# A new emission order for a fused attention and Fourier-filter kernel: same operations, other order, other PSUM banks, other clamp pairs

## The chip, the cores and the metric

One core of one Trainium2 chip runs the whole program. The metric is the device time of one execution in microseconds (us); the median of several runs is compared. The profile is one execution taken by the hardware profiler. Its engines are PE (TensorE matmul; PEld its weight loads), DVE (VectorE), ACT (ScalarE), POOL (GpSimd) and SP (SyncE, which here only issues transfers).

## The reference

One batch of 2048 tokens, 448 features, bf16. Two branches of the same input are mixed by a gate for each token.

```python
x = A_x                                                   # [1, 2048, 448]
g = sigmoid((x * gate_w).sum(-1, keepdims=True))
q, k, v = split(x @ wqkv)                                 # 16 heads of 28
a = (softmax(q @ k.T * 28**-0.5) @ v) @ wo                # full attention
X = rfft2(x.astype(f32), axes=(-2, -1)) * (w_r + 1j * w_i)
b = irfft2(X, s=(2048, 448)).astype(bf16)
return g * a + (1 - g) * b
```

## The kernel before, in words

**Attention.** Four heads make a group `g`, 512 queries a block `c`; the 16 pairs (g, c) are worked off in a fixed sequence `n` = 0 to 15. For a pair, 16 key tiles `kt` of 128 keys are scored: a score matmul is [32 rows] x [128 keys x 512 queries], on one of four row tiles of TensorE (one for each head `s`), into one PSUM bank. A unit is one (n, kt, s).

There are two ways from a score to a probability. Most key tiles ("a" tiles) take ACT: one `ACTIVATE` of line 1111 takes the exponential of two units at once (128x1024) into a slot pair of `ring`. I call one such pair a step; there are 374, numbered 0 to 373, all two units wide. The last 3 to 5 key tiles of a pair ("d" tiles) take DVE and POOL: score matmuls named `dunit`, then a clamp on DVE (line 1061, `dp1`) that writes bf16 bits as integers into `pd`, then three `int64_add` on POOL (line 1075, `dexp`) that make three phase-shifted copies. A clamp takes one unit, or a pair of units in neighbouring banks; `PARTS` lists the ways in which the four units of a d tile can be split, and one byte of the table picks one for each of the 69 d tiles.

A `pv` operation is four matmuls on the four column tiles of TensorE (values x probabilities), added up in one PSUM bank `pvb`. When a pair (g, c) is done, `normalise` copies the bank out (line 1241), and a chain of small transfers and a reciprocal brings the row sums back for the last multiplication (line 1253): transfer 0 (`rs`), reciprocal, transfer 1 (`rsc`), four broadcasts 2 to 5 (`Rb`). For n = 15 that is done on TensorE instead.

**The rest**, fed in between: transposes of x (`x_block`), projections (`proj_group`; the squared norms go to `nrow` and by a small transfer into a row of `k` or `q`; in each of them a matmul `:4` makes the norms), values (`v_block`), their weights (`w_block`), and the Fourier branch: `fwd`, `fwd2`, sixteen `mid` (each loads seven pieces, `CS` and six of `Wg`), sixteen `inv` (each loads `V`). Then sixteen output tiles: `out_tile` 0 to 11 and `last_tile` 12 to 15, each eight column-tile operations (four of the Fourier branch, four of the attention), an eviction, and a store. `out_tile` t writes one of two buffers `fin`, so its eviction waits until the store of tile t-2 has landed.

Seven PSUM banks (`ps`) are handed out one by one to scores, clamps and the rest; the eighth is `pvb`.

**What sets the order.** `Sched.run` emits the operations in the order of a table. The engines work in program order, so the table fixes the order on each engine's queue (PE, DVE, ACT, POOL, and SP's transfer queue); waits between engines follow from the data. `TABLE` holds four compressed strings: `codes` (the operations' numbers in order of emission), `banks` (the PSUM bank for each item), `widths` (units in a step) and `parts` (the split of each d tile). `Kernel.passed` tells the framework which of the earlier `dexp` instructions a new clamp or `dexp` need not depend on ("product done": the `pv` that read it has passed).

Some names of the diff and of the text: `S` a score, `D` a dunit, `P` a pv operation, `O` an output-tile operation, `i` one of `inv`, `J` a projection. "Row work" is S and D (row tiles), "column work" is P, J, `fwd`, `mid`, O (column tiles), "full" are `v_block`, `inv` and transposes (the array as one tile).

Of the kernel before, what the change touches and what calls it, by code (L numbers as in the profile page):

```python
# [21 lines left out]
S, D, H, DH, F = 2048, 448, 16, 28, 225  # L22
# [16 lines left out]
    "eNoN14MCIDoSRNEkHXNs27Zt27Zt27Zt27Zt2zbe7P5E1bkKtUQaGdQUORQFRUXRUHQUA8VEsVBsFAchFBfFQ/FRApQQJUKJURKUFGGUDKVDyVF2"  # L39
    "lAJZlBLlQAR1RRJ5JBCg9CgVYigrSo0iIY6qozQoA0qLqqEaqArKgjKhnKgyiohyocwoG6qFMqLiqASKjEqimig3Ko0CioDKoLooD8qL8qECKD8q"  # L40
    "gsqiUqg8KogKocKoKNqEyqHNqAIqhlqhtmgL2opWonZoG9qOVqHVqBLagdagiWgtqogmocloHVqPpqCpaAPaif5jf9lv9ottRBTVQfVQQ9QbNUI9"
    "0TTUEXVC7VEz1AI1QVVRG9Qc/WH/2HQ0A81Es9BsNAfNRfPQfLQALUSL0GK0BC1FsXBsHAcvQ3FxPBwfJ8AJ8S4UEUfCkXEUHBVHw9FxDLwcJcIx"
    "8QqEOeK70R60F+1D+9EBRDnwp+gZeo5eoJfoFXqN3iDOBX+LCGdc8oNIc8UdtzzwCPwQuoPuonvoPnqAHqJH6DEy3POIPDFOgpPiZPgJeofeow/o"
    "I0qOP6HPqLarjQ6jSDwyj8qj8al4Gp6OZ+CYPAafiaPw6LyBPoKOomPoOPqC6uo4PDaPxU+guDwF/opS4ng8Pk/IE/E6OgFPzFPhU+g0OoPOonPo"
    "PLqALqJL6DK6gq6ia+g6uoFuom8oNW6MTqLW6Ba6jZLwpLwULo3L4BQ8OU/NU/GyOBlPydPgtDgd/o5+oJ/oF0qPf6MMuBwuj5vqhjoRJIa0PB2v"
    "pyvgNDwmZOAZeXRIzzPxxroijgFZeGbeXCeAyJCdZ+NZeQ4eCxJCR9wJ5+I5eVTojLvgKBANuuK8PA9PArl5Pp4ZZ8FZcTacHefAOXEunJ8X4PEg"
    "KVTC9VF8+Iv+oIy4D8qEu6G4EAeSQXJIAbEhN86D8+J8OD8ugAviQvg/9A8V4oU5whgTDJjigrwIL8qL8eI8PTDMscASK6yxwRY7XBgXwUVxBvA4"
    "4Ai4BC/Ju+MeuDQvw8vznrgXLsXL8nK8Iq/EW+u2ugTujUvi4rgYrsKr8pa6Mm6vq+CquBquwCvzarwGr85TQ21ek7fSzXRaqMWb6EY6DVTH6aAe"
    "r8tTQjaowzvoBjwHNOTtdAtdnzfi2SEVZIEmvDEfiUfhnJAVauBmvDnPBaPxGJwbmvI2uiVvxVvw1rwm7qjH4va8LW/DO/D6uh3vyGvhOrgurofr"
    "48yQFzqgfNALZYKM0Bn1QHmgC+qkB+rCUAg68068AS4CfXRvXQK68a68lquNO+suvDsfrofqHrwnLwd9dWUoCVWgD+/Nh+lBeoDuxfvy8lAV+vMy"  # L50
    "0I/31wP5IF4A8sMAPkIP1kP4UN5Fl4WC0Bq3wSP4cD6YD+MjeSloi9vhhjCKj+ZjeHEoDRWgPR6nG8EQPUrXh3F8LK8Bdd0EPpHXc/VdA1cJuqMG"
    "UBPG80l8Cp/MZ/GZvKFr5Bq7hrir7qZ76Gi+p+6ue+mxehqfzifoqXwGn80b4ca4KW6GW7vmeA6fyxtDG9cEWuCRuiIUhfm8BSzg8/gU3U8v5ot4"
    "NRitx+upeppuiRfyJbwDbgmtcHVYxpfyutAGVvCVvJ1r7ybpDq6jm6g1LOf1oC2s4+v5ar6GT9ar+Fq+gReDMbo21IHmUAuaQjPo5Dq7Pni6boIb"
    "oBm6rYvqB+MheCgehofjLq6J28g38c28qWvmmrtluh1s5Vv4Ar1Ud4UdfDtfqVfrbbyFa+m6Q3to5XrALr6br9HdoCfs5Hv4Pr6X7+etYJFerA/w"
    "g/wQbw393Qbd1XWGI/wwH+C6OQNdYKHu4Xq6Xu44P8YHwlG+RC/XJ3l/OMV7uxP8NF+hz/IzvBseBH3xWt3HDYC+rh/u587zC3yQG+xW6SFuqDvH"
    "L/NL/CK/yq/xK/w6H+PGunFuvNuuF+JFeDFegoe54W6Em+AmuknuJr/BB8NS3Ac6QS/oABv1Jn2b3+EjYQTs0lv0Zn2L3+X3+H0+BEbBHXwX38P3"
    "8QP8kD/iT/kT/hA/wo/xE/wUP8PP8Qv8Er/Cr/ED/pg/4yvwSrwKr8Zr8Fq8Dq/HG/BGvAlvxlvwVrwNb8fP+QveF17ycXimtjACO3iDZ+EdeDye"
    "gF/zV3winoT7wWQ80o1y7/hbPgne8Pd8r96mx8JH/oHv0Ov0ZJgCX/g0+Mw/8a98HEyH5bgjDIXesFOv18NgOHzj3/lomAFTYQzMhN36F//Jt+p9"
    "eo+egifCeJgDE+AH/83/8b/8D18MszES8+G//4/Nfj0HL4AlcEJf0QuBCBCn9Dl9Us8FJrg4qxc4KhbBGpBCCSG0WOgWucXuop4Ha2EFWGHEDX1Z"
    "n9FeBLEdnIgglriVsNQtc9PcdDfDzXSbIaKIJHbAbX1aRxFRxTqILKKJKH4Axr4/nqUj+9l6jp6rB+LubgGejwfhufiAnqfn4b9utFsKy2EWzIZl"  # L60
# [64 lines left out]
    "w33y7uZf/hf7bvjyhBu8Ts6vfm85QIy/yMohVurrn72vq8u7v1dD/uk4+uRxIJ9chFrL5Xf6RQGPIbgOoXupUuXjTCymQQNFr2kowqRmG0XzoPHS"  # L125
    "i6JBSQbcGfFk5AzRG6MnJOUndz09Msq5d8QGMkUpGDANHy/OD6bzDdc=",
# [1419 lines left out]
```

## Time and profile before

| | |
|---|---|
| median of 3 runs | 380.56 us (380.28 to 380.94) |
| the profiled execution | 380.92 us, span 379.0 us |
| first ACT step starts, last one ends | 12.67 us, 365.58 us |
| ACT line 1111 | 374 instructions, busy 345.6 us, idle before them 7.3 us |
| PE busy | 367.8 us (97%) |
| DVE busy | 336.6 us (89%) |
| POOL busy | 234.9 us (62%) |
| granted clock | 0.999 |

How to read it: a step of ACT lasts 1.02 us or more in the records, but the next one begins before it ends, so the pace is read from starts, not from durations. The same holds for PE: the ends of matmuls are modelled, and the distance of starts tells what an operation costs. The span lies 1.9 us below the profiled execution's own time, and that execution lies 0.36 us above the median.

### The profile page before, as it was taken

Reading aid. Unit: us, or ns where it says so; the run is one execution under the profiler, and the core shown is the slowest. Engines: PE = TensorE matmul, PEld = TensorE weight load, DVE = VectorE, ACT = ScalarE, POOL = GpSimd, SP = SyncE. Lnnn points to the kernel's source line nnn. Section 1 sums busy time; section 2 is a strip of 40 time slices with the busy share of each in tenths; the row PEclk is TensorE's granted clock in tenths of the full one; section 3 lists DMA queues with packets and bytes.
Section 4 is the critical chain, followed back from the end, with each engine's and each line's share of the span. In section 5 each row is a group of like instructions: output and inputs, shape, how many; then the busy total and the mean of one; then the engine's idle time right before and its main releaser. Section 6 shows DMA issues by size and latency. Waiting matters only on the chain.

```text
span 379.0 us, 12133 instructions
## 1 busy us (share of the span) xinstructions
PE 367.8 (97%) x5093; PEld 144.0 (38%) x5093; DVE 336.6 (89%) x649; ACT 350.6 (92%) x389; POOL 234.9 (62%) x264
## 2 busy tenths in 40 slices
PE   8999999999999999999999999999999989999995
PEld 5644233343333332334334434233333333433563
DVE  1769889999999999999999999999999989996644
ACT  2799999999999999999989999999999999999741
POOL 4707295747878876483463556877877759654610
PEclk9999999999999999999999999999999999999999
DMA  6601001001201122113211212212313222222122
GB/s 145 171 3 45 3 5 47 21 6 39 60 15 31 47 57 52 51 38 99 68 38 39 70 36 73 59 39 64 80 41 80 66 48 80 70 67 72 48 78 88
DMA packets 31154, 21.20 MB, mean 56 GB/s; under 512 B 16260, under 2 KB 29052, under 8 KB 31100
## 3 DMA queue, kind: packets, MB, share of 16 engines
q1 hardware_dynamic: 29708, 19.96, 20.0%
q8 instruction: 40, 0.66, 0.7%
q10 hardware_dynamic: 1392, 0.46, 0.5%
q14 instruction: 14, 0.11, 0.1%
HBM read 14.51 MB, written 1.96 MB: 43 GB/s over the span
## 4 chain that ended last, share of the span: by engine, by line
PE 49%; ACT 41%; DVE 5%; SPq 1%; issue 1%; DMA 1%; POOL 0%; DVEq 0%; POOLq 0%
ACT ring L1111 41%; PE ps L500 32%; PE pvb L500 16%; DVE pd L1061 3%; SPq L475 1%; PE ps L503 1%; DMA out_dram<-wpk 1%; DVE X L1373 0%; DVE pvs L1241 0%; DVE t L1437 0%; DMA Wg<-in_B_w_r_dram 0%; ACT V L1321 0%; DVE wpq L1299 0%; DVE wpk L1299 0%; DVE Ab L1390 0%
## 5 line engine op out<-in xcount | busy, mean ns | idle before, releaser
L1111 ACT ACTIVATE ring<-ps 128x1024 bf16<-128x1024 f32 x374 | 345.6, 1135 | 7.3 <-PE ps L500 7.1
L1075 POOL INT64_ADD pd<-pd x207 | 213.0, 1044 | 107.2 <-DVE pd L1061 32.3
L1061 DVE TENSOR_SCALAR pd<-ps 128x512 uint16<-128x512 f32 x260 | 177.2, 715 | 6.1 <-PE ps L500 3.8
L500 PE MATMUL ps<-q,k 32*128 32x512 bf16 x1024 | 143.7, 382 | 4.3 <-ACT ring L1111 1.5
L500 PE MATMUL pvb<-pd,vd 128*32 128x512 bf16 x1104 | 94.8, 384 | 0.0
L500 PEld LDWEIGHTS <-k 32*128 32x128 bf16 x1024 | 40.9, 91 | 118.1 <-issue 113.2
L500 PE MATMUL pvb<-ring,vw 128*32 128x512 bf16 x748 | 68.8, 384 | 0.4 <-DVE pvs L1241 0.4
L500 PEld LDWEIGHTS <-vd 128*32 128x32 bf16 x1104 | 24.3, 95 | 33.1 <-issue 27.8
L500 PEld LDWEIGHTS <-vw 128*32 128x32 bf16 x748 | 17.5, 94 | 25.3 <-issue 22.4
L500 PEld LDWEIGHTS <-xT 128*128 128x128 bf16 (+5 forms) x512 | 19.4, 97 | 10.8 <-issue 9.9
L1437 DVE TENSOR_TENSOR t<-ps,Wg 128x450 bf16<-128x450 f32 x32 | 19.0, 619 | 1.5 <-PE pvb L500 1.0
L500 PE MATMUL ps<-xT,wpq 128*32 128x512 bf16 (+3 forms) x248 | 19.4, 382 | 0.3 <-DVE wpq L590 0.3
L500 PE MATMUL ps<-xT,wpk 128*32 128x512 bf16 (+3 forms) x244 | 18.4, 383 | 0.0
L1373 DVE TENSOR_TENSOR X<-ps,oc 128x226 bf16<-128x226 f32 (+1 forms) x32 | 12.2, 385 | 0.6
L500 PE MATMUL ps<-wvr,xT 128*128 128x112 bf16 (+1 forms) x192 | 12.7, 213 | 0.0
L500 PEld LDWEIGHTS <-CS 128*32 128x32 bf16 x384 | 8.8, 95 | 9.5 <-issue 5.2
L804 DVE TENSOR_SCALAR q<-ps 128x512 bf16<-128x512 f32 x15 | 10.3, 684 | 2.3 <-PE ps L500 2.3
L500 PE MATMUL ps<-wpk,q 128*32 128x448 bf16 x128 | 11.7, 362 | 0.0
L500 PE MATMUL ps<-wpq,q 128*32 128x448 bf16 x128 | 11.5, 362 | 0.0
L500 PE MATMUL ps<-Bd,xT 128*32 128x226 bf16 (+2 forms) x256 | 11.1, 263 | 0.3 <-ACT ring L1111 0.3
L1494 DVE TENSOR_TENSOR X<-ps,ogb 113x512 bf16<-113x512 f32 x16 | 10.3, 674 | 1.2 <-PE ps L500 1.2
L804 DVE TENSOR_SCALAR k<-ps 128x512 bf16<-128x512 f32 x15 | 10.3, 684 | 0.9 <-PE ps L500 0.8
(99 smaller groups left out, 270.5 us busy)
## 6 DMA issues: line engine op xcount, KB each, us to landing
Rb<-rsc SPq DMA_DIRECT2D x60, 64.0 KB
CS<-cCS SPq DMA_DIRECT2D x16, 192.0 KB
V<-xtok SPq DMA_DIRECT2D x16, 113.0 KB
Wg<-in_B_w_i_dram SPq DMA_DIRECT2D x64, 28.1 KB
xtok<-Ab SPq DMA_DIRECT2D x16, 112.5 KB
xtok<-in_A_x_dram SPq DMA_DIRECT2D x3, 448.0 KB
Wg<-in_B_w_r_dram SPq DMA_DIRECT2D x32, 28.1 KB
out_dram<-wpq SPq DMA_DIRECT2D x6, 112.0 KB
```

The costliest lines, as they stand in the source:

```text
L475: self.pin(e.dma_start(out=out() if callable(out) else out, in_=in_() if callable(in_) else in_))
L500: self.pin(self.nc.tensor.matmul(out, lhsT=lhsT, rhs=rhs, start=start, stop=stop, **kw))
L503: self.pin(self.nc.tensor.transpose(out=out, in_=in_, identity=self.c("ident")[0:n, 0:n]))
L804: self.pin(nc.vector.tensor_scalar(out=dst, in0=self.bgi(it), scalar1=SQ, scalar2=None, op0=ALU.mult))
L1061: self.pin(nc.vector.tensor_scalar(out=free_dims(ys[:], [[512 * e, w], [1, 512]], 512 * part[0]).bitcast(U16), in0=self.ps[:, bs[0]:bs[0] ...
L1075: self.pin(nc.gpsimd.int64_add(out=fl(pds), in0=fl(ys), in1=PHASE[f] * 0x0001000100010001))
L1111: self.pin(nc.scalar.activation(out=self.ring[:, u0:u0 + len(st), :], in_=self.ps[:, bs[0]:bs[0] + len(st), :], func=ACT.Exp, scale=LN2 / ...
L1373: self.pin(nc.vector.tensor_tensor(out=free_dims(self.X1[:, t, :], [[F, 2], [-1 if dif else 1, n]], (F - 1) * dif), in0=free_dims(self.bgi ...
L1437: self.pin(nc.vector.tensor_tensor(out=out[:], in0=self.bgi(it)[:, 0:F2].rearrange("p (a f) -> p a f", a=2), in1=free_dims(Wg[:], [[F, 2], ...
L1494: self.pin(nc.vector.tensor_tensor(out=free_dims(self.zt[0:FN], [[128, 4], [1, 128]], 512 * t), in0=self.bgi(it)[0:FN, :].rearrange("p (a ...
```

## The change

The source is the same but for the table and one condition in `passed`:

```diff
 TABLE = (
-    "eNoN14MCIDoSRNEkHXNs27Zt27Zt27Zt27Zt2zbe7P5E1bkKtUQaGdQUORQFRUXRUHQUA8VEsVBsFAchFBfFQ/FRApQQJUKJURKUFGGUDKVDyVF2"
...
+    "eNoN14MCIDoSAMFkYq9t27Zt27Zt27Zt27Zt28bbu6+oboVaIo0MaoocioKiomgoOoqBYqJYKDaKgxCKi+Kh+CgBSogSocQoCUqKMEqG0qHkKDtK"
...
     "eNpjYhoF9AcAJW4C7Q==",
-    "eNpjYGBgYGRgYWDgBBF4AAsnUAkEcHBycrKBGBABFhYACYkAYw==",
+    "eNoti0EOACAMwrpkc/L/DytTAqEHgIQJwShlfz0I6k7a2FtoSU25fI08EEkArQ==",
 )
@@ passed
-                                       keep=[p for p in self.copies if self.taken.get(p.name, o.at) >= o.at])
+                                       keep=[p for p in self.copies
+                                             if p is self.before.get(ins.engine) or self.taken.get(p.name, o.at) >= o.at])
```

Decompressed and read against the list of operations, the tables say this. `widths` is the same string: 374 steps of two units, so ACT's work is the same. `parts` differ: 54 d tiles of 69 were clamped unit by unit before, 41 are after; 260 clamps (244 of one unit, 16 of two) become 245 (214 and 31). All other operations are the same set, 3997 before and 3982 after. The first 69 PE operations and the first 12 transfers of SP are the same. ACT's order differs only in where seven small instructions stand (the weights' exponentials). On PE 2026 of 2377 operations stand at another place, by 3 places in the median and 90 at most; on SP 283 of 316.

Runs of row work on PE (stretches of S and D with nothing else between) are 328 before and 322 after. By stretches of steps, counted in the emission order from the last score of one step to the last score of another:

| steps | row runs before / after | column operations | full operations |
|---|---|---|---|
| 0 to 8 | 5 / 6 | 13 / 11 | 48 / 55 |
| 8 to 64 | 49 / 51 | 113 / 114 | 60 / 56 |
| 64 to 152 | 83 / 80 | 199 / 202 | 69 / 69 |
| 152 to 193 | 34 / 37 | 101 / 97 | 36 / 36 |
| 193 to 208 | 11 / 12 | 43 / 46 | 27 / 20 |
| 208 to 312 | 95 / 92 | 202 / 202 | 73 / 80 |
| 312 to 320 | 8 / 7 | 18 / 17 | 0 / 0 |
| 320 to 360 | 37 / 36 | 85 / 84 | 48 / 48 |
| 360 to 373 | 7 / 6 | 68 / 63 | 12 / 12 |

PE near the last steps, before (the number after S is the step):

```
i(4) P O4(0-7) i(8) S363 S364 P O3(0-7) P P P S365 S366 D D O6(0-7) P S367 D D P P O5(0-6) S368 S369
O8(0-5) P O5(7) O8(6-7) O10(0-2) P S370 S371 O7(0-3) O10(3) O7(4) O10(4) P O7(5) P O10(5-7) S372 S373 ...
```

and after:

```
i(12) P P O4(0-5) S363 S364 O4(6-7) P P O3(0-7) S365 S366 D D P P O6(0-7) P S367 S368 D D P O5(0-3) P O5(4-7) P S369 S370 S371
P O10(0-2) P P O10(3-5) O7(0-7) O10(6) S372 S373 ...
```

Behind step 373 PE has 18 `out_tile` operations and 7 pv operations left before, 25 and 6 after; the `last_tile`, `inv` and `normalise` operations there are the same.

SP's queue after its twelfth transfer, before: `wk` part 2, `wq` part 2, `A`, `wk` part 1, the norm row of k block 1, k block 2, k block 3, ... After: one `Wg` piece and the `CS` of `mid` 1, then `wq` part 2, `wk` part 1, `wk` part 2, the norm row of k block 1, `Bd`, a `Wg` piece, k block 2, half of `wvr`, k block 3, ... (`wk` and `wq` are the raw weights of groups 1 to 3.) On POOL, the copy that completes the values' weights of block 0, which the first pv operation needs, stands 18th of POOL's operations before and 30th after, now behind six copies that unpack those raw weights.

For `mid` 14 and 15 SP's queue holds, before, 14 pieces with three loads of the output weights and one other transfer among them; the piece loaded last is a `Wg` of `mid` 15. After, it holds the 14 pieces with two such loads, and the `CS` of `mid` 14 is last but one.

Near the end DVE's order is, before: evictions of `out_tile` 4, 3, 6, 5, 8, 10, 7, 9, 11; after: 4, 3, 6, 5, 7, 8, 9, 10, 11. The stores on SP follow, before: 4, 6, 3, 8, 5, 7, 9, 10; after: 4, 3, 5, 6, 8, 7, 9, 10.

More of the change, by code (lines that the diff above doesn't have):

```diff
@@ L44 @@
[L44 to L48, printed above, removed]
@@ L124 @@
[L124 to L126 removed]
+    "eNoN14MCIDoSAMFkYq9t27Zt27Zt27Zt27Zt28bbu6+oboVaIo0MaoocioKiomgoOoqBYqJYKDaKgxCKi+Kh+CgBSogSocQoCUqKMEqG0qHkKDtK"
+    "gSxKiXIgQF2RRB4JRFB6lAoxlBWlRpEQR9VRGpQBpUXVUA1UBWVBmVBOVBlFRLlQZpQN1UIZUXFUAkVGJVFNlBuVRgFFQGVQXZQH5UX5UAGUHxVB"
@@ new lines @@
+    "ZVEpVB4VRIVQYVQUbULl0GZUARVDrVBbtAVtRStRO7QNbUer0GpUCe1Aa9BEtBZVRJPQZLQTTUFT0Wv2hr1n71gv1BN1RH1QQ9QMUfSWfWC70Do0"
+    "Hc1AM9F6NAvNRhvQHDQXzUPz0QK0EC1Ci9EStBQtQxFxJBwZx8KxcRwcF8fD8XECHAVHxQlxNBwdx8Ab0XK0An1lX9hH9ontRnvQXrQPJcIx8X50"
+    "AH1m39kP9o39ZL/Yb/aHHUT/sb/sHzuEnqJn6Dl6gV6iV+g1eoPuoLvoHrqPHqCH6BF6jI6go+gYQhzz4+gteoIS4yT4HXqPPqCP6AQCzjz4eqg2"
+    "qoMOo9KOcsIF5zwpToZbo0aoMeqAOqHmqBs6iVqgJmgaqoqm4ml4Op6BP6HkWHPFGZfc8M/oCzqFTqMz6CyaiVPgr8hxyyvqCDzwstrziDwljswj"
+    "8XPoPLqALqJL6DK6gq6ia+g6uoFuolT4FrqNovGoPCaPwcvpKDw6T4PT4nQ4Pf6OfqCf6BfKgH+jz+4bqo9S41K4NC6Dy+L4PB6Pw2Pzcrg8Lq+r"
@@ new lines @@
+    "6Vg8Lk/AY5JKOiFPxBPzWKQCrqITkCQ8OknKa+iKOCFJRFLw5DwZT8ljkMSkI+6EO+PIJBVPzbvgqCQtT8fT8PS8jGuAKuEopCuORjLjLDgrzoaz"
+    "4xw4J87AM/J4JBfOjfPgvDgfzo8L4IK4EI5PkpDMPAvPxLPy/9A/hDDGgAmmmOHsPBvnWGCJFdbYYIsdzsEL46SkCC6K/6Le6A+KSzLh5KQLikM6"
+    "oxQkJ8/Fu+N0JC/Pw3PzfLwH7ol7YY8DjoDTkwI8P6+li/JivBAvzAvyIrw3rqMr4yq4Kq6Gi+ESuIGuoFOSVKQkL8GL81K8JK6OU5PiuLqup8vw"
+    "0rymzkoyk3K8PK+q6+u6uiyvwLORLKQKr8Qr8jSkKq/MM+LYJBmpgdOSkXgUHo3H4JwkO6nOa/BqvCZvpCvrWrw2b6hr67E4F2nIG/B6vC6vw+vz"
+    "RjwHqYnr4Lq4Hq6PM5EMJC9pjzKSPCQ3aYN6oMa6Fm7CG/NmvI3upJvzQqQAqY2b6HeuKW/B2+ouugEuSAqT8qQVb8nb6x66o27Lq5CqpA1vpzvr"
@@ new lines @@
+    "1rwdr0CqkSKkA2/PO/KeuoMuSjrxzjwf6apLk268Ky9LuvDuXJP8pCEuR1rjNrgtbod78h68JOmuy5BSpATpzfvw/roRbo+Lke6oEqlMipOKpDHu"
+    "xfvyAbqca0D68f68mx7EB/JGZAAfzMu7IbqCq+gakqF8CG9MhumaZDgfwYfxkbySq+yquG64Fumtm+JmuB4ZzUfx5rgFrk7G8bF8DB/P65OWuAOu"
+    "QfrgVni4Hqgn8Im8n67jJvMpvAmZzifxqbyPHqqn8Zaklx6k67qmpBWZyduSWXyw7qtn8Nl8Lp/D5/MFfB5fyNuREbq+a+AaukausWviBuOqrpqr"
+    "7mq4mq6WG4IX80V8KJ6mh+HapC5pQZqROqSpq+2G4/ZkKV/Gp+slfI7uRlbwlXw5X8U7kO5ksu5BVvM1vBfpi2fqnqQ1WcfX80l6ol7LN/GNfAPf"
+    "zHuTDm6WbkP64Y7OkBG4C9nCt/KBZK7ewbfzZm6q3sZ38t18F9/Du5JBpLmboVu6Vq61a+P28b38AD/I9/NDfJ6eovu6fq6z6+L6uwGunhuIm2ru"
@@ new lines @@
+    "m+AvjvpB+IMbqdu6dq69a6YHukGuq+vmVusjfDA5zFfo4/wYP8pP8CFksOvuerierjmZrZfohXgRXoyX4KX4FD/Jh5K+ZAzqTDqSPqQTWaQX635k"
+    "NDnDz/JRZL5eqIeRMeQ0P8fP8wv8Dr6L7+H7+AF+iB/hx/gJfoqf4av8Gr/ML/Hn+AV+iV/h1/giv8Kv8xV4JV6FV+M1eC1eh9fjDXgj3oQ34y14"
+    "K96Gt+ObvD+5wZvrVrqlbqE7OUtm4VHakXH4DR6PJ+Db/A6fiCfhHXgAaa0n4yn4Pr/Hb/G7/AHv5Zbrlfohf8SnkwW6t5tBJpOn/AmfSh7zZ3wK"
+    "WarX6WX6BX/Ox5Gx5CUfTkaSEWQaGU9W6Vf8NV9A1ur1eo1eSD7yd/wtn0k+8A16FnnD3/NPfDbeqXfrJeQLX0Q+8+V4EplLJpBleCKZQ+bgpWQx"
+    "2af362/8O59HzuiJbpKb7Ka4r/wn/8V/8N98LZlPDukD+g//y1eSXfqIln60HoA36vduHh6vF+D+eD5u4ebiMXqcHqununVkmltF/nEkdpA9+qT+"
@@ new lines @@
+    "jxMBAgsqtpCdZLob7ka4kW6UW/9/hJjYSjaQ0W6MO4VP4zP4LD6Hz+ML+CK+hC/jK1gJKVaTNWSsE+KoNsIKLZy4iq/h6/gGvolnk2VkORmEDutA"
+    "NhMvgthG9urT+haOQG7j7WQFiSgiiV0kqogidpMIIrKIJnbiXXg33oP34n14Pz6AD+JD+DA+go/iY/g4PoGji1gitoghPuC3+B2eoE/imCKOuKDP"
+    "6yHuhL6sT+mjJK6IJ67pYzqhSCAOkqHuGDmu44sz5AJJIhKLRCKpOETOkqVumVvuDuoVLrlIJk6RjWQf2Uuu6LN6E9lDLpKV7jRZ5Q6TVCKlSCGu"
+    "6ut6P0kr0ojUIp24qM/pS/oIWe0OkAwivThHbpHMIpPIKLKIG/o8uU1Oksf6ob5Bsops4pF+oa+RqySnyCFe6bf6Pb5JNunrJLvILfKIXCKveKJ3"
+    "ul1ut9vjCol8Ir/4pt/rh6SgKCAKi71un9vvjpNL5Kle5IqIouI+eamf6WFus76p+7gteqsm/hFZ7J6QEqK4eEwekKekmCgpPunZbo6b6+a5UqK0"
@@ new lines @@
+    "hofeQTjt8tp8Nr8tYAvaQjaNTqvT6ww6nc6oC9si1rjgHpsn5ql5Zp6bF+aleWU220emqP1tt9jXJpPOrLPprPoJe8ay6Ozaugiuoq1kK9sqtqqt"
+    "ZqvbGjaye86esmL2jcmjc+scOqd+xB6ymvYxy6Xz6oiuuC1hS9pS1rnStowta8vZqK68fcliuxfsFcun8+tCuqAuoovqArqwLqaVO2lP2dP/n/do"
+    "7ow9a8/Z2raOrWvr2fq2gW1oG9nztoQurkvrUrqkLqO32uhum91ud9iddpfdbffYKC6ti+Fiukiugq1l/9j/7IjQ2P61e+0++88i18TGcuncZXvB"
+    "XrFX7TV73d6wN+0tG8fFdSPDqDA6jAljw357wB60h+xhe8QetcdsYpfEJXXxXHx33J6w6V0yl8FldMldQVfIFXYpXAKX0GGX0qVymVx2d9Emcqnd"
+    "bZvD5XSZXS6XxeV2eVxel88VcUVdMVfclXD53SWbxt2xBVxWl82VdKXc/wAj5xFm",
@@ L127 @@
+    "Bd1Jh4eyzFaH/kYGHUX3oVUXl0/GNgdlphfp+lK7mALw1WVSS9OicCg1vz5IfEg8/gGZbQ3M",
     "eNpjYhoF9AcAJW4C7Q==",
-    "eNpjYGBgYGRgYWDgBBF4AAsnUAkEcHBycrKBGBABFhYACYkAYw==",
+    "eNoti0EOACAMwrpkc/L/DytTAqEHgIQJwShlfz0I6k7a2FtoSU25fI08EEkArQ==",
 )
```

135 lines of the change are left out of this document (55 added, 80 removed).

## The prediction

> **What bounds the kernel now.** I read the page first: which engine has no room left.
>
> ```profile
> PE 367.8 (97%) x5093; PEld 144.0 (38%) x5093; DVE 336.6 (89%) x649; ACT 350.6 (92%) x389; POOL 234.9 (62%) x264
> L1111 ACT ACTIVATE ring<-ps 128x1024 bf16<-128x1024 f32 x374 | 345.6, 1135 | 7.3 <-PE ps L500 7.1
> L1075 POOL INT64_ADD pd<-pd x207 | 213.0, 1044 | 107.2 <-DVE pd L1061 32.3 <-PE pvb L500 22.8 <-DVE sq L809 18.1
> ```
>
> Three engines are nearly full. ACT has one fixed train of 374 steps, and what it waits for is PE's scores. So I ask, stretch by stretch, how far the train runs behind its own best pace. This is the view of busy time in stretches, for line 1111 alone; the stretches begin at the starts of steps 0, 8, 64, 152, 193, 208, 312, 320 and 360 (a count in brackets takes in the step that overlaps the left edge).
>
> ```profile
> core 0: us, ACT busy (x), PEclk, DMA share, GB/s
> 12.67:21.34 8.67, 7.65 (x8) 1.00 0.38 84
> 21.34:72.99 51.65, 51.65 (x56) 1.00 0.08 22
> 72.99:153.81 80.82, 80.82 (x90) 1.00 0.16 41
> 153.81:192.69 38.88, 38.08 (x43) 1.00 0.20 55
> 192.69:208.25 15.56, 14.20 (x16) 1.00 0.15 41
> 208.25:303.46 95.21, 95.21 (x105) 1.00 0.25 61
> 303.46:311.37 7.91, 7.62 (x9) 1.00 0.22 51
> 311.37:348.11 36.74, 36.70 (x40) 1.00 0.21 66
> 348.11:365.58 17.47, 13.67 (x15) 1.00 0.25 74
> 365.58:379.00 13.42, 0.00 (x0) 0.97 0.24 81
> ```
>
> Steps 208 to 312 are the smooth stretch: 95.21 us for 104 steps, 0.9155 us a step; that is ACT's pace. Against it the others are late by 8.67 - 8 x 0.9155 = 1.35 us (0 to 8), 0.38 (8 to 64), 0.25 (64 to 152), 1.35 (152 to 193), 1.83 (193 to 208), 0.58 (312 to 320), 0.12 (320 to 360), and 17.47 less a last step of 1.02 less 13 x 0.9155, 4.55 (360 to the end). In all 10.4 us; that is the most that an order can win between the first step and the last. The remaining 13.4 us are the tail, with no step in it.
>
> Why it is late is read from ACT and PE in order of time.
>
> ```profile
> 351.73 1.94 ACT L1111 ACTIVATE ring<-ps 128x1024 bf16<-128x1024 f32 x2 [0.67 <-PE ps L500]
> 354.23 3.10 ACT L1111 ACTIVATE ring<-ps 128x1024 bf16<-128x1024 f32 x3 [0.55 <-PE ps L500]
> ...
> 363.64 1.94 ACT L1111 ACTIVATE ring<-ps 128x1024 bf16<-128x1024 f32 x2 [1.01 <-PE ps L500]
> ```
>
> ```profile
> 315.13 0.55 PE pvb L500 x8
> 315.67 0.32 PE ps L500 x3
> 316.00 0.33 PE pvb L500 x4
> ...
> 320.35 0.76 PE pvb L500 x12
> ```
>
> The second fence is the chain of work that ended last. One pv operation (x4) between score groups takes 0.33 us, two 0.55, three 0.76: each further one 0.217, and the turn from column tiles to row tiles 0.11. A group of scores and dunits takes 0.32 with its turn, whether it holds 2, 3 or 4 matmuls. So PE's cost lies in the number of row runs and of column operations, not in the number of scores. A step is late when PE's work since the last scores is over 0.9155 us, or over twice that where two steps' scores stand together. Example: between S364 and S365 PE does one output tile (1.2 us) and four pv, 2.46 us with the turns, for two steps; ACT's rows show 354.23 - 351.73 = 2.50 for those two steps instead of 1.83.
>
> **The change part by part.**
>
> *PE's turns.* The same column and full operations, 328 row runs before and 322 after, and 676 changes of tile mode before, 663 after. Six row runs less at 0.217 and 13 turns less at 0.11 are -2.7 us of PE. How much of it reaches ACT depends on where it lies. I went through both orders step by step with the prices above (a Fourier output operation 0.10, an attention one 0.20), counting as lateness what a step's work has over 0.9155 and over a lead. A lead is one step where two steps' scores stand together, and at most 0.3 us otherwise; with 0.3 the smooth stretch comes out smooth (0.19). Lateness in us:
>
> | steps | measured | counted before | counted after |
> |---|---|---|---|
> | 0 to 8 | 1.35 | 1.55 | 0.93 |
> | 8 to 64 | 0.38 | 0.82 | 0.25 |
> | 64 to 152 | 0.25 | 0.57 | 0.73 |
> | 152 to 193 | 1.35 | 1.15 | 0.67 |
> | 193 to 208 | 1.83 | 1.48 | 1.38 |
> | 208 to 312 | 0 | 0.19 | 0.06 |
> | 312 to 320 | 0.58 | 0 | 0 |
> | 320 to 360 | 0.12 | 0.20 | 0.29 |
> | 360 to 373 | 4.55 | 3.78 | 3.49 |
>
> The count gives 9.7 of the measured 10.4, so it names the places well. Its difference is 9.74 - 7.80 = **-1.94 us**. The turn's price can be argued: the Trainium skill, "TensorE: Matmul & The Clock Gate", section "Step-by-step: what each phase is for", says that a matmul's drain of 128 cycles is hidden under the next matmul's fill; if a turn only exposes it, that is an estimate of 0.05 us a turn. The rows show 0.11; with the page's price the 13 turns would save 0.7 instead of 1.4 and the sum would be about -0.8 in place of -1.5. The rows decide.
>
> *The opening.* The norm row of k block 1 is needed by step 8.
>
> ```profile
> 17.12 0.38 PE L500 MATMUL ps<-sq,cst 128*32 128x512 bf16 x1
> 18.24 0.66 SPq L475 DMA_DIRECT2D k<-nrow  x1
> 20.91 0.40 PE L500 MATMUL ps<-q,k 32*128 32x512 bf16 x4
> ```
>
> From the norm matmul to the first score that uses the row it took 3.79 us, of which 2.67 from the issue, though PE was busy all that time, so 2.67 is an upper bound. After, the norm matmul stands one step's scores later (behind S5). In its place I expect it at 17.1 still, because its bank is freed by step 3; so step 8 cannot start its scores much before 20.7. Of the counted -0.62 I take -0.25 (**+0.37**; ends 0 and 0.62). The Trainium skill, "DMA: Bandwidth & Descriptors", section "Anatomy of one DMA — SWDGE (gpsimd) path", gives about 2.0 us as a transfer's fixed cost; by that the row would be there at 20.2, the whole 0.62 would come, and the sum would be about -1.9. The trace has no wait that ends on the landing of such a row.
>
> *The late Wg in steps 312 to 320.*
>
> ```profile
> 296.99 0.54 SPq L475 DMA_DIRECT2D Wg<-in_B_w_i_dram  x1
> ...
> 307.26 0.59 SPq L475 DMA_DIRECT2D Wg<-in_B_w_r_dram  x1
> 309.54 0.63 DVE L1437 TENSOR_TENSOR t<-ps,Wg 128x450 bf16<-128x450 f32 x1 [0.99 <-PE pvb L500]
> ```
>
> SP issues a piece each 0.6 us, the last `Wg` of `mid` 15 goes out at 307.26, and DVE's product starts 2.28 us later after 0.99 us idle (the row names PE; the load issued last fits better, its issue ending at 307.85). That is the 0.58 that my count doesn't have. After, the products of `mid` 15 stand some two steps later and fewer foreign loads stand in the batch; but the `CS` of `mid` 14 is last but one. Before, the first piece that had to wait for `mid` 13's products went out at 296.99; after, the first such piece has eleven behind it up to that CS, so the CS goes out at 296.99 + 11 x 0.6 = 303.6 and lands, by 2.28, at 305.9. PE wants it behind the scores of step 315, which starts at 303.46 + 3 x 0.9155 = 306.2; scores start 0.43 ahead of their step (20.91 against 21.34 above), and last 0.3, so at 306.1. It is in time by 0.2 us. I take **-0.3** (ends -0.58, and +0.6 if the CS is late by as much as the Wg was).
>
> *Stores near the end.*
>
> ```profile
> 356.88 0.43 SPq L475 DMA_DIRECT2D out_dram<-wpk  x1
> 360.20 0.72 DVE L1299 TENSOR_SCALAR wpk<-ps,glog 128x448 bf16<-128x448 f32 x1 [2.03 <-DMA out_dram<-wpk]
> ```
>
> `out_tile` 5's eviction waits 2.03 us until the store of tile 3 has landed, 3.3 us after its issue; DVE is blocked, and banks come back late: of the 4.55 us, 0.77 are not in the count. After, tile 3 is evicted some steps before tile 5's matmuls end, so that wait goes. Next late is tile 9: its eviction waits for the store of tile 7, which is now issued behind four `Rb` loads and the store of 8; on DVE, the last normalisation's product (`normalise` 15) stands behind it. PE has some 1.2 us of `last_tile` work to cover that. I take **-0.4** (ends -0.77 and +0.6).
>
> *The tail.* Behind step 373 PE has 7 `out_tile` operations more and one pv less.
>
> ```profile
> 372.86 0.57 PE L500 MATMUL ps<-wpk,q 128*32 128x448 bf16 x8
> 373.25 0.38 PE L500 MATMUL ps<-wpq,q 128*32 128x448 bf16 x4
> 373.65 0.57 PE L500 MATMUL ps<-Bd,X 113*32 113x224 bf16 x16
> 374.03 0.39 PE L500 MATMUL ps<-wpq,q 128*32 128x448 bf16 x4
> 375.07 0.76 ACT L1321 ACTIVATE V<-ps,glog 128x448 bf16<-128x448 f32 x1 [1.00 <-PE ps L500]
> ```
>
> An attention operation takes (373.25 - 372.86)/2 = 0.20, a Fourier one (374.03 - 373.65)/4 = 0.10. Counted over the two orders the PE work from the last scores to the last operation is 11.17 before and 11.92 after: **+0.75**. PE works through to 375.0, and ACT's last eviction waits for it, so this is on the path. (Ends 0, if the chain of normalise 15 set the tail, and +0.75.)
>
> *Without cost.* 15 more pairs of clamps: two single clamps take 1.29 us, a pair 1.21,
>
> ```profile
> 354.43 1.29 DVE L1061 TENSOR_SCALAR pd<-ps 128x512 uint16<-128x512 f32 x2 [0.44 <-PE ps L500]
> 356.37 1.21 DVE L1061 TENSOR_SCALAR pd<-ps 128x1024 uint16<-128x1024 f32 x1
> ```
>
> so DVE has 15 x 0.08 = 1.2 us less to do, spread over 350 us; a pair also gives its first bank back later. I take 0 (ends -0.3 and +0.3). The new condition in `passed` only keeps an order between neighbours on POOL, which works in order; should each of the 207 copies pay something, POOL's 107 us of idle time cover it.
>
> *Sum.* -1.94 + 0.37 - 0.3 - 0.4 + 0.75 = **-1.5 us**: the profiled execution's 380.92 (its span and 1.9 us around it) would be 379.4, and the median, which lies 0.36 lower, **379.0 us**.
>
> **The rivals.**
>
> *Slower: the raw weights come late.* A `CS` (192 KB) and a `Wg` now stand ahead of them on SP.
>
> ```profile
> 9.11 2.06 SPq L475 DMA_DIRECT2D X<-in_A_wqkv_dram  x2
> 16.32 0.37 POOL L593 COPY wpq<-X 96x224 bf16<-96x224 bf16 x1 [0.43 <-DMA X<-in_A_wqkv_dram]
> 21.24 0.62 PE L500 MATMUL ps<-xT,wpq 128*32 128x512 bf16 x8
> ```
>
> Before, the loads issued from 9.11 on let POOL go at 16.32, some 6 us after the issue of the second: the queues are full then. After, they come 1.2 us later by two more issues, and by up to 220 KB / 84 GB/s = 2.6 us (the rate of the first stretch above): landing at 17.5 to 20.1. The unpacking of `wq` for the q projection is the fourth and fifth copy, 0.37 each, so done 1.8 later, 19.3 to 21.9, and the values' copy at 20.0 to 22.6. PE wants the first at about 21 (21.24 before), the second by step 12, near 23. So PE stands still for 0 to 0.9 us, and all of that is lost to ACT. To end slower by 0.2% the wait must reach 1.5 + 0.76 = 2.3 us, which it does if the loads land after about 21.5. For it: the 6 us; against: that rate is a mean over a stretch that holds idle time too. With 2.5 us it gives 379.0 + 2.5 = 381.5.
>
> *No change.* The two stretches that hold 6.4 of the 10.4 us (193 to 208, 360 to 373) change by 0.39 only in the count; the rest of the gain lies in part where the count is above the measured (8 to 64: 0.57 of a measured 0.38). With half of the gain outside those two, (-1.94 + 0.39)/2 = -0.8, with the 0.39, no gain from the two late transfers, and the tail's 0.75: -0.4, 380.1 us.
>
> *Much faster.* All of the transfers' waits go (-0.58 and -0.77), the opening comes whole, the tail's 0.75 hides: -3.3 us, 377.3. I count it in the forecast's sign.
>
> **How the numbers follow.** Within 0.2% (0.76 us) is about what a measurement can't tell from no change. The forecast and its better case (faster by more than that) 0.60; no change 0.22; slower 0.18. Eight in ten: from 0.3 below the better case, 377.0, to the slower rival with its loads half a us later still, 382.0. The forecast's own range is 377.3 to 379.8.
>
> **What would show it.** Right: the last ACT step ends near 363.3 instead of 365.6, and the tail is 14.2 instead of 13.4; the lateness of steps 193 to 208 stays near 1.7; DVE's 0.99 idle before a product and the 2.03 before `out_tile` 5 are gone. Wrong: if ACT's first eight steps are later than 21.3 or POOL waits for `X` longer than 0.43; if PE waits for `CS` near step 315; if steps 320 to 360, smooth now, are not; or if `normalise` 15 waits behind tile 9 and the tail is over 15 us.

## The result, and the profile after

The changed kernel takes 382.41 us (median of 16 runs, 381.62 to 384.75) against 380.56 us before (16 runs beside it): a ratio of 1.0061, 95% interval 1.0043 to 1.0079. It is slower by about 2 us where 1.5 us less was forecast. The profiled execution took 383.24 us, its span 381.4. The first lines are those of the page that answer to before's:

```profile
PE 369.5 (97%) x5093; PEld 143.7 (38%) x5093; DVE 336.1 (88%) x634; ACT 351.2 (92%) x389; POOL 233.6 (61%) x264
PEclk9999999999999999999999999699999999999999
L1112 ACT ACTIVATE ring<-ps 128x1024 bf16<-128x1024 f32 x374 | 346.3, 1123 | 9.7 <-PE ps L501 9.3
```

The totals say little: the engines do nearly the same work as before, and ACT idles 2.4 us more. The second line does say something: one slice in 40 has the clock at 0.6. Next the view of busy time in stretches, for ACT's line alone (now 1112), cut at the starts of the same steps as in the prediction:

```profile
11.77:20.55 8.78, 7.62 (x8) 1.00 0.57 155
20.55:72.23 51.68, 51.64 (x56) 1.00 0.06 16
72.23:153.58 81.35, 81.07 (x89) 1.00 0.14 36
153.58:192.85 39.27, 38.18 (x42) 1.00 0.21 49
192.85:208.29 15.44, 14.15 (x15) 1.00 0.17 39
208.29:306.87 98.58, 95.89 (x105) 0.97 0.26 63
306.87:314.17 7.30, 7.30 (x10) 1.00 0.13 34
314.17:351.23 37.06, 36.87 (x42) 1.00 0.22 68
351.23:367.64 16.41, 13.63 (x15) 1.00 0.23 76
367.64:381.40 13.76, 0.00 (x1) 0.95 0.26 86
```

With the same 0.9155 us a step, steps 208 to 312, which were smooth, are now late by 98.58 - 95.21 = 3.37 us, and the mean clock there is 0.97. (The span is longer by 2.4 us: 3.0 of lateness and 0.34 of tail, less 0.90 because the first step of this execution starts at 11.77 and not at 12.67. In a_rb57 below, with the same opening order, it starts at 12.69, so the early start is one execution's.) What happened stands on DVE and PE, in order of time:

```profile
189.87 0.69 DVE L1254 TENSOR_TENSOR q<-pvs,Rb 128x512 bf16<-128x512 f32 x1 [0.84 <-DMA Rb<-rsc]
235.81 0.69 DVE L1254 TENSOR_TENSOR q<-pvs,Rb 128x512 bf16<-128x512 f32 x1 [1.33 <-DMA Rb<-rsc]
```

```profile
191.21 0.39 PE L501 MATMUL ps<-q,k 32*128 32x512 bf16 x3 [0.46 <-DVE pd L1062]
...
237.15 0.37 PE L501 MATMUL ps<-q,k 32*128 32x512 bf16 x1 [0.71 <-DVE pd L1062]
239.85 0.90 PE L501 MATMUL ps<-q,k 32*128 32x512 bf16 x4 [0.38 <-DVE pd L1062]
```

Twice DVE stands still before the last multiplication of a `normalise` (5 and 7), because an `Rb` broadcast has not landed. Clamps are queued behind it, the banks that they free come late, and PE waits for them. Before, the product of `normalise` 7 started without a wait:

```profile
230.16 1.20 DVE L1253 TENSOR_TENSOR q<-pvs,Rb 128x512 bf16<-128x512 f32 x1
```

SP's queue shows why (first before, then after):

```profile
226.38 0.58 SPq L475 DMA_DIRECT2D Rb<-rsc  x1
```

```profile
228.92 0.59 SPq L476 DMA_DIRECT2D Rb<-rsc  x1
...
232.44 0.43 SPq L476 DMA_DIRECT2D Rb<-rsc  x1
232.91 0.54 SPq L476 DMA_DIRECT2D Wg<-in_B_w_r_dram  x1
233.50 0.58 SPq L476 DMA_DIRECT2D Rb<-rsc  x1
```

Before, the last of `normalise` 7's four pieces went out at 226.38 and its product started at 230.16, 3.8 us later. After, the four are spread among eight pieces of `mid` 6 and 7 and a load of output weights, with SP issuing without a pause; the last goes out at 233.50. The product would have had its turn at 235.81 - 1.33 = 234.48; it starts 2.31 us after the issue, when the piece has landed.

Behind the second wait comes a thing that the profile of before does not show while the steps run: a dip of the clock (of the 79 executions of before beside the experiments 78 have a mean clock of 0.998 or more, and the one with 0.949 took an ordinary 380.69 us). The view of stretches for PE (its length, PE's busy time and count, the clock, the transfers):

```profile
236.60:240.00 3.40, 2.46 (x25) 1.00 0.20 55
240.00:246.60 6.60, 6.60 (x50) 0.50 0.23 58
246.60:250.00 3.40, 3.40 (x50) 0.97 0.09 26
```

After 3.4 us in which PE was busy for 2.46, the granted clock is 0.50 for 6.6 us and a little more. Of the 16 executions six have a mean clock of 0.995 or less; their median is 384.4 us, that of the ten others 382.2. So the executions with a dip take 2.2 us more, and those without it are still 1.6 us slower than before. That the dip alone costs the 2.2 us is argued, not shown: these executions may also have had the longer waits.

### The profile page after: what moved, and what is told of

Read it like the earlier page. It is cut to its first block, busy times and chain, and to the rows that moved or that the text cites. A ratio compares the mean times of both kernels' runs of the same rounds, so it can differ in the third digit from the quotient of the medians.

```text
span 381.4 us, 12096 instructions
## 1 busy us (share of the span) xinstructions
PE 369.5 (97%) x5093; PEld 143.7 (38%) x5093; DVE 336.1 (88%) x634; ACT 351.2 (92%) x389; POOL 233.6 (61%) x264
## 4 chain that ended last, share of the span: by engine, by line
PE 57%; ACT 35%; DVE 5%; SPq 1%; DMA 1%; issue 0%; POOL 0%; DVEq 0%; POOLq 0%
PE ps L501 37%; ACT ring L1112 35%; PE pvb L501 19%; DVE pd L1062 2%; SPq L476 1%; PE ps L504 1%; DMA Rb<-rsc 1%; DVE X L1374 0%; DVE q L805 0%; DVE q L1254 0%; DVE t L1438 0%; DVE sq L810 0%; ACT V L1322 0%; DVE oc L1370 0%; DVE xT L773 0%
## 5 line engine op out<-in xcount | busy, mean ns | idle before, releaser
L1062 DVE TENSOR_SCALAR pd<-ps 128x512 uint16<-128x512 f32 (+1 forms) x245 | 176.1, 751 | 7.4 <-PE ps L501 5.8
L501 PE MATMUL pvb<-pd,vd 128*32 128x512 bf16 x1104 | 97.5, 389 | 0.1
L501 PEld LDWEIGHTS <-k 32*128 32x128 bf16 x1024 | 39.9, 91 | 118.2 <-issue 113.0
L501 PE MATMUL ps<-wvr,xT 128*128 128x112 bf16 (+2 forms) x192 | 13.2, 213 | 0.0
L1254 DVE TENSOR_TENSOR q<-pvs,Rb 128x512 bf16<-128x512 f32 x15 | 10.2, 679 | 2.2 <-DMA Rb<-rsc 2.2
```

Source lines behind the costliest of these rows:

```text
L501: self.pin(self.nc.tensor.matmul(out, lhsT=lhsT, rhs=rhs, start=start, stop=stop, **kw))
L1062: self.pin(nc.vector.tensor_scalar(out=free_dims(ys[:], [[512 * e, w], [1, 512]], 512 * part[0]).bitcast(U16), in0=self.ps[:, bs[0]:bs[0] ...
L1254: e = self.dve(dv(512), lambda: self.pin(nc.vector.tensor_tensor(out=dst, in0=pvs[:], in1=self.Rb[:], op=ALU.mult)), ds, kk, lk=True)
```

## The experiments

`MOVES` below is a small addition to `Sched`: each entry takes transfers out of the table's order and puts them behind another one; nothing else is touched. Every ratio is to executions of before taken beside that experiment.

```diff
+        for run, behind in MOVES:
+            self.codes = [c for c in self.codes if c not in run]
+            i = self.codes.index(behind) + 1
+            self.codes[i:i] = run
```

**a_rb7**, the changed kernel, `normalise` 7's pieces first:

```diff
+MOVES = (
+    ((3712, 138, 3709, 3706,), 2935),    # mid 7's pieces and a load of output weights: to the end
+    ((2936, 3686, 2937, 2935,), 3692),   # Rb, CS of mid 6, Rb, Rb: forward
+)
```

> The changed kernel, with SP's transfers near step 230 in another order: the four Rb broadcasts of normalise 7 ahead of the pieces of mid 7. Theory L (a late broadcast): in the changed kernel DVE idles 1.33 us before the product of normalise 7, because its last Rb piece is issued at 233.50; clamps behind it come late, PE idles 0.71 and 0.38 us, and in the profiled execution the granted clock is 0.50 for some 6 us behind that. With the pieces issued at about 229 the wait of DVE and PE's two waits go, the granted clock is 1.00 throughout, steps 208 to 312 are late by under 0.3 instead of 3.37 us, and the time falls from 382.4 to between 380.9 and 381.4 us. Theory P (PE's own order is the loss, the wait hides elsewhere): the wait goes, the time stays between 382.0 and 382.6.

Measured: 380.86 us (380.14 to 381.65, 11 runs; before, beside it, 380.28), ratio 1.0015 (1.0003 to 1.0027). Steps 208 to 312 are late by 0.04 us, and the clock is 0.998 or more in every run. `normalise` 5 still waits, and longer than in the profile after:

```profile
191.28 0.69 DVE L1264 TENSOR_TENSOR q<-pvs,Rb 128x512 bf16<-128x512 f32 x1 [1.51 <-DMA Rb<-rsc]
```

```profile
192.62 0.40 PE L511 MATMUL ps<-q,k 32*128 32x512 bf16 x3 [1.12 <-DVE pd L1072]
```

So theory L holds for this place, theory P falls. PE stood still for 1.12 us here without any dip of the clock.

**a_rb57** adds one more line:

```diff
+    ((2860, 2862,), 2861),               # normalise 5: two Rb pieces behind the first ones
```

> As a_rb7, and two Rb pieces of normalise 5 ahead of six pieces of mid 2 and 3 and others. Theory L: DVE's 0.84 us before the product of normalise 5 goes, and PE's 0.46 and 0.20 us near 190 to 192 with it; steps 152 to 193 are late by 1.0 instead of 1.74 us; 0.5 to 0.8 us faster than a_rb7, 380.2 to 380.8. Theory P: within 0.2 us of a_rb7.

Measured: 379.86 us (379.02 to 380.76, 12 runs), ratio 0.9985 (0.9973 to 0.9997). That is 1.0 us below a_rb7, a little more than expected, as the wait was 1.51 and not 0.84. DVE's waits for `Rb` are gone:

```profile
153.58:192.85 39.27, 38.18 (x42) 1.00 0.21 49
```

(steps 152 to 193 after, as above), and in a_rb57

```profile
154.50:192.98 38.48, 37.88 (x42) 1.00 0.21 49
192.98:208.34 15.36, 14.22 (x16) 1.00 0.17 41
208.34:303.60 95.26, 95.26 (x105) 1.00 0.27 66
...
347.96:364.38 16.42, 13.63 (x15) 1.00 0.25 75
```

That is 38.48 us for 41 steps, late by 0.95 us (worked out before rounding). A few transfers that change places on one queue are worth 0.0076 of the time, and the changed kernel becomes faster than before.

**a_oldcond**, the new table with the old condition:

```diff
-                                       keep=[p for p in self.copies
-                                             if p is self.before.get(ins.engine) or self.taken.get(p.name, o.at) >= o.at])
+                                       keep=[p for p in self.copies if self.taken.get(p.name, o.at) >= o.at])
```

> The changed kernel with the condition in passed as it was before (new table, old condition). Theory C (the condition is the loss: each of POOL's 207 copies waits for the one before it): faster by over 1 us, at most 381.4 us. Theories L and P: the order on POOL is the same with or without it, so 382.2 to 382.7 us, with DVE's 1.33 us before normalise 7's product still there.

Measured: 383.1 us (382.32 to 385.52, 6 runs), ratio 1.009 (1.006 to 1.012). Theory C falls. The time also lies above the 382.2 to 382.7 of theories L and P. The dip came in two of the six runs (mean clock 0.987 and 0.991), and DVE's wait at `normalise` 7 was 2.19 us in the profiled one. The time lies above that of the changed kernel too, with overlapping intervals; the next test asks the condition alone.

**b_newcond**, the kernel before with the new condition (the same lines, the other way round):

> The kernel before with the new condition in passed alone (old table). Theories L and T: nothing to be seen, 380.1 to 380.5 us. Theory C2 (the condition helps: the changed kernel without it was 383.1 against 382.4): faster by 0.3 to 0.7 us, 379.6 to 380.0.

Measured: 380.88 us (11 runs; before 380.5), ratio 1.0002 (0.9991 to 1.0014). The condition does nothing that can be measured with the old table.

**b_late7**, the kernel before with one broadcast made late:

```diff
+MOVES = (
+    ((2949,), 3721),                     # an Rb piece of normalise 7 behind the CS of mid 7
+)
```

> The kernel before, with one Rb piece of normalise 7 issued five places later on SP (behind the CS of mid 7, at about 229.5 instead of 226.38 us). Theory L: it lands at 231.8, DVE idles 1.2 to 2 us before the product that now starts at 230.16, and the time rises by 0.7 to 1.6 us, to 381.2 to 382.2, and more in executions where the granted clock drops. Theory P: DVE waits and PE's banks cover it, 380.4 to 380.9 us.

Measured: 382.88 us (381.96 to 383.75, 6 runs; before 380.28), ratio 1.0067 (1.0049 to 1.0085). One transfer, five issues later, makes a kernel slower by as much as the whole change did (the intervals overlap), and by more than I expected. The piece went out at 230.26; DVE, PE and two stretches of PE's time:

```profile
232.69 1.18 DVE L1262 TENSOR_TENSOR q<-pvs,Rb 128x512 bf16<-128x512 f32 x1 [1.97 <-DMA Wg<-in_B_w_i_dram]
```

```profile
234.63 0.65 PE L509 MATMUL ps<-xtok,CS 128*32 128x450 bf16 x12 [1.56 <-DVE vt L950]
```

```profile
231.00:235.00 4.00, 2.43 (x42) 1.00 0.27 76
235.00:238.40 3.40, 3.40 (x35) 0.50 0.08 17
```

(The row of DVE names a `Wg` load issued at about the same time; the product reads `Rb`.) Here the clock is at half for 3.4 us; four of the six runs have a mean clock of 0.996 or less. The two others took 381.96 and 382.10 us, 1.7 and 1.8 us above before, so most of the loss is there without a dip.

**b_late3**, the same piece, moved by three places:

```diff
+    ((2949,), 3705),                     # behind a Wg piece of mid 6
```

> The kernel before, with the same Rb piece of normalise 7 moved by three places instead of seven (behind a Wg piece of mid 6), so that it goes out at about 229.0 and lands 2.4 us later at 231.4. Theory L with a cover: DVE waits about 0.7 us (1.97 in b_late7), PE idles under 0.5 us, the granted clock stays at 1.00, and the time rises by 0 to 0.6 us, 380.3 to 380.9. Theory G (any wait of DVE there costs PE as much, and PE's idle time lets the clock drop): 381.0 us or more, with a stretch at half the clock in the profile.

Measured: 380.39 us (12 runs; before 380.5), ratio 1.0004 (0.9992 to 1.0016).

```profile
230.14 0.69 DVE L1262 TENSOR_TENSOR q<-pvs,Rb 128x512 bf16<-128x512 f32 x1 [0.49 <-DMA Wg<-in_B_w_r_dram]
```

DVE waits 0.49 us and nobody behind it notices. So DVE has a cover here of about half a microsecond at least, and of less than the 1.97 of b_late7. Between no loss and 2.6 us lie two places on SP's queue (three and five; the "seven" of the expectation is a slip).

**b_two**, the kernel before with its own two late places mended:

```diff
+MOVES = (
+    ((139, 131,), 3882),                 # two loads of output weights behind the last Wg of mid 15
+    ((3067,), 3265),                     # the store of output tile 3 ahead of that of tile 6
+)
```

> The kernel before, with three of SP's transfers moved: two loads of the output weights behind the last Wg piece of mid 15, so that this goes out at about 304.8 instead of 307.26 us, and the store of output tile 3 ahead of that of tile 6, at about 354.1 instead of 356.88. Theory T (the transfers are the whole difference; PE's new order, the banks and the clamp pairs are worth under 0.3 us): steps 312 to 320 go from 0.58 to under 0.1 us of lateness, DVE's 2.03 us before output tile 5 go and steps 360 to 373 fall from 4.55 to 3.7 to 4.0; the time falls to between 378.9 and 379.4 us, at least as low as the changed kernel with its broadcasts mended (379.86). Theory O (the new order of PE is worth 0.5 us or more beside the transfers): this kernel stays above that one, 379.8 us or more, because PE is full there and the waits come back elsewhere.

Measured: 379.83 us (379.08 to 380.34, 11 runs; before 380.5), ratio 0.9979 (0.997 to 0.9987). The old order with three transfers moved is as fast as the new order with its broadcasts mended (0.9985, 0.9973 to 0.9997). That comparison is what theory T says. Its time isn't met: 378.9 to 379.4 us were expected, the gain is 0.8 us (0.0021), and 379.83 lies at the edge of theory O's 379.8 or more, whose condition, staying above a_rb57, isn't met either. So T holds as a comparison, not in its size. The reason lies in the kernel before itself. Its `Wg` wait of 0.58 us was not there in two other profiled executions. b_newcond, and b_late3 with the same order from there on, have the stretch 312 to 320 at

```profile
303.80:311.13 7.33, 7.33 (x9) 1.00 0.24 60
```

```profile
302.87:310.24 7.37, 7.37 (x9) 1.00 0.21 51
```

0.01 and 0.05 us late. The wait for the store of tile 3 is there each time (b_late3, then b_two, where the wait has become one for PE):

```profile
359.40 0.73 DVE L1308 TENSOR_SCALAR wpk<-ps,glog 128x448 bf16<-128x448 f32 x1 [2.36 <-DMA out_dram<-wpk]
```

```profile
358.80 0.75 DVE L1309 TENSOR_SCALAR wpk<-ps,glog 128x448 bf16<-128x448 f32 x1 [1.29 <-PE ps L510]
```

and steps 360 to 373 take 17.47 us in before, 17.99 in b_newcond, 17.80 in b_late3 and 17.07 in b_two. So b_two's gain is the store's.

**h_ba152, h_ab152, h_bab**: spliced orders. At the exponential of step 152 the two tables have emitted nearly the same set of operations, so that the rest of one can follow the beginning of the other; an operation keeps the bank and the clamp split of the table that it comes from. The edit itself replaces the table's strings; this is how the new `codes` are made (h_ab152 the other way round, h_bab with two seams):

```diff
-codes = NEW
+codes = OLD[:i] + [c for c in NEW if c not in OLD[:i]]   # i: where OLD emits exp 152 (h_ba152)
```

> A spliced order: the old order up to the exponential of step 152, from there on the new order with its broadcasts mended (as in a_rb57). Theory M (what counts is the lateness that the trace measures by stretch: 1.97 us in steps 0 to 152 of the old order, 2.65 in the new): 0 to 152 come out late by 1.9 to 2.1 us, the rest as in a_rb57, and the time is 0.4 to 0.9 us below a_rb57's: a ratio to the kernel before of 0.9960 to 0.9975. Theory K (the count of the prediction: the new order is better by 1.03 us there, 0.66 with the opening's correction): 0.3 us or more above a_rb57's, a ratio of 0.9993 or more.

> The mirror image: the new order up to step 152, from there on the old order with the three transfers of b_two moved. Theory M: 0 to 152 late by 2.5 to 2.7 us, the rest as in b_two; 0.4 to 0.9 us above b_two, a ratio to the kernel before of 0.9990 to 1.0005. Theory K: 0.3 us or more below b_two, a ratio of 0.9971 or less.

> Three pieces: the old order to step 152, the new one (broadcasts mended) from 152 to 320, the old one with the store of output tile 3 moved from 320 on. Theory M: each piece brings its own lateness: 1.97, then 2.6 to 2.8 in steps 152 to 320 (the old order has 3.2), then 0.1 and 4.1 to 4.5; in all about 0.5 us less than b_two, a ratio to the kernel before of 0.9955 to 0.9975, the lowest of all. Rival S (at the seams the transfers come late, since each order has its own queue on SP): DVE or PE waits for a transfer within 20 steps of a seam, and the ratio is that of b_two, 0.9979, or above.

Measured beside one another (before 380.67): h_ba152 380.33, ratio 0.9991 (0.9982 to 1.0); h_ab152 380.22, 0.9993 (0.9979 to 1.0007); h_bab 380.68, 0.9998 (0.9988 to 1.0008). h_ab152 comes out where theory M has it and theory K has not; h_ba152 comes out 0.0016 above M's range, near K's, though not for K's reason; h_bab is above M's range too. Theory M has the stretches from 8 to 152 right and fails at what follows the seam. (Steps 0 to 8 of h_ba152 are late by 2.26 us and not 1.35: in that execution the first step starts at 11.68 instead of 12.67, and step 8 at 21.27, near the 21.34 of before.) Steps 64 to 152, then 152 to 193, in h_ba152 and in h_ab152:

```profile
72.92:153.73 80.81, 80.81 (x89) 1.00 0.15 38
153.73:192.87 39.14, 38.00 (x42) 1.00 0.18 48
```

```profile
72.98:154.33 81.35, 81.06 (x90) 1.00 0.16 39
154.33:193.12 38.79, 38.03 (x43) 1.00 0.22 55
```

From 64 to 152 each piece has its own lateness (0.25 in the old, 0.78 in the new order). But the new order's 152 to 193, late by 0.95 us behind its own beginning, is late by 1.61 behind the old one. What the old order saves before the seam is paid behind it. The mirror image wins 0.09 us there (1.26 for 1.35). The three pieces of h_bab bring nothing either: steps 320 to 360 are 0.70 late where both parents have 0.11 and 0.44. Neither DVE nor PE waited for a transfer near a seam, so rival S isn't the reason, though its ratio is met. I read it as work of PE that is put off and not avoided; that is argued, not shown.

## Why the prediction was wrong

Lateness by stretch in the profiled executions, by the prediction's own formula (old order: before, b_newcond, and b_late3 with its one moved transfer):

| steps | old order | counted after | after | a_rb57 | b_two |
|---|---|---|---|---|---|
| 0 to 8 | 1.34, 1.35, 1.35 | 0.93 | 1.46 | 1.46 | 1.41 |
| 8 to 64 | 0.38, 0.38, 0.38 | 0.25 | 0.41 | 0.41 | 0.38 |
| 64 to 152 | 0.25, 0.25, 0.25 | 0.73 | 0.78 | 0.78 | 0.25 |
| 152 to 193 | 1.35, 1.35, 1.35 | 0.67 | 1.74 | 0.95 | 1.35 |
| 193 to 208 | 1.83, 1.84, 1.83 | 1.38 | 1.71 | 1.63 | 1.84 |
| 208 to 312 | 0.01, 0.16, 0.00 | 0.06 | 3.37 | 0.05 | -0.01 |
| 312 to 320 | 0.58, 0.01, 0.05 | 0 | -0.03 | -0.03 | 0.01 |
| 320 to 360 | 0.12, 0.11, 0.11 | 0.29 | 0.44 | 0.44 | 0.11 |
| 360 to 373 | 4.55, 5.07, 4.88 | 3.49 | 3.50 | 3.50 | 4.15 |

- **The missing term.** This is the step that failed. The failure of sign is a term that the sum did not have, so that it stood at nothing without a reason: the broadcasts of `normalise` 5 and 7. By the ratios, a_rb7 to a_rb57 is 0.0030 (1.1 us) and after to a_rb7 is 0.0046 (1.7 us), together 2.9 us, the clock's dips included. I looked for late transfers where the trace of before had one (`Wg` of `mid` 15, a store) and where the queue's head had changed (raw weights, a norm row), but 283 of 316 transfers had moved. The check that I made for the `CS` of `mid` 14 (place on SP x 0.6 us, plus 2.3 us to land, against the turn of the reader) gives the answer for `Rb` too: 233.5 + 2.3 = 235.8 against a turn at 234.5 (by the issue times of after, which would have had to be worked out from the order).
- **PE's turns, -1.94.** Wrong in size. Leaving out steps 360 to 373, the count promised -1.65 us; a_rb57 against the middle one of the old executions has +0.11, +0.03, +0.53, -0.40, -0.20, +0.04, -0.08 and +0.33, in all +0.36. One fault was to subtract two counts: that of before lay 0.76 above the measured in steps 8 to 152, so it promised gains that were not there to be had. The rival "no change" had said so. The other fault is the count of the new order itself. It is fair in three stretches (0.25 for 0.41, 0.73 for 0.78, 3.49 for 3.50), but in all it has 7.80 where a_rb57, without the late broadcasts, measures 9.19; 0.53 of that is missing in steps 0 to 8, 0.28 in 152 to 193 and 0.25 in 193 to 208. Measured before against counted after would have given -0.97 for the same stretches without 312 to 320, where a_rb57 has +0.44: nearer, and still of the wrong sign.
- **The opening, +0.37.** I took -0.25 with the correction; it came out at +0.11, outside both ends. The mechanism wasn't the one given. The norm row did not hold step 8 back: in a_rb57 it was issued at 18.52, and PE worked without a pause until the scores at 21.04, 2.52 us later. What the count lacks is in the main two waits of PE for DVE, ahead of the norm matmul and at it: 0.27 and 0.18 us in a_rb57, 0.28 and 0.18 in after, where before has none. As for the 2.0 us of the page, the section of the Trainium skill that the prediction names is about transfers that GpSimd issues, and SP issued this one.
- **The late `Wg`, -0.3.** The lateness went to zero, as predicted, and was worth next to nothing, since the 0.58 was one execution's: two others have 0.01 and 0.05.
- **The stores, -0.4, and the count's -0.29 there.** Right in mechanism, too small: 4.88 to 3.50 is -1.38. b_two shows that the store alone is 0.73 of it, close to the 0.77 that I had as the end.
- **The tail, +0.75.** Right for PE: from the end of the last step to the start of PE's last operation it is 374.64 - 365.58 = 9.06 us before, 9.83 after and 9.82 in a_rb57. The whole tail varies by what follows: 13.42 before, 13.76 after, 14.32 in a_rb57.
- **At no cost.** The condition: shown with the old table (b_newcond); with the new one a_oldcond only shows that it isn't the loss. The clamp pairs and the banks were not tried by themselves; with the broadcasts mended the whole new table is worth -0.6 us, so they hide nothing large unless something else makes up for it.
- **The slower rival** had the right sign and the wrong transfer. Its premise came true, and cost nothing:

```profile
17.85 0.37 POOL L591 COPY wpk<-X 128x224 bf16<-128x224 bf16 x1 [2.84 <-DMA X<-in_A_wqkv_dram]
```

The raw weights landed at 17.85, within the 17.5 to 20.1 given, but PE had other work in front of the q projection and waited for none of it. Two of the prediction's signs of being wrong came, this wait of POOL (2.84 us) and the steps 320 to 360 (0.44 late); none of its signs pointed at `Rb`.

The terms that were right sum to little: with both broadcasts mended the new order stands at 0.9985 where -1.5 us would be 0.996, and b_two has the same from one store.

## What to carry to other kernels

When an order is changed, go through every transfer that has moved and not only those that were late: issue time on its queue, plus the landing time that the trace shows, against the turn of its reader; where DVE waited for a broadcast here, it started 2.2 to 2.4 us after the issue (2.20 in b_late3, 2.31 in after, 2.43 in b_late7), so a margin under some 2.5 us on this queue is to be looked at. A wait of DVE can cost nothing up to the cover behind it (0.49 us in b_late3) and most of its length beyond (1.97 us in b_late7, of which 1.7 to 1.8 were lost in the runs without a dip); between these two nothing was tried. A model's count for the new order is set against the measured old one, not against the model's count for it, and even then it has only the waits that the model knows. And a wait that is seen in one execution is first looked for in a second one.

## What the runs showed of the hardware

The granted clock fell to 0.50 in the middle of a kernel that keeps PE busy. The traces also keep the times at which the clock switched. Half clock lasted 6.83 us in the profiled execution of after and 3.41 us in that of b_late7. In all twelve traces the time between two switches is a whole multiple of 3.413 us: 69, 2 and 39 times in after, 67, 1 and 42 in b_late7, 109 or 110 times in those without a dip. So the clock is set on a fixed grid of windows of that length. The Trainium skill, "TensorE: Matmul & The Clock Gate", section "Part 1: The HAM clock gate (the "warmup" mystery)", gives a free-running window of 3413 ns; the traces agree with that length. The table of that section of the Trainium skill has the half clock after at least one idle window. In the window ahead of the drop PE was here busy for 2.46 us of 3.41 (72%) in after and for 1.84 (54%) in b_late7, so a window that is idle in part was enough.

The busy time alone does not decide it. In the profiled execution of a_oldcond PE is busy for 2.13 us in each of two such windows, from 190.27 and from 238.06, and only the second is followed by half clock. The changed kernel's own wait lowered the clock in six of 16 executions, and PE's wait of 1.12 us near 192 us in a_rb7 in none of 11. What else decides is not shown.
